# Softmax's division is applied to x as it leaves PSUM, with factors spread over rows by DMA; GpSimd takes over parts of the q and k preparation

## The chip, the cores and the metric

One core of one Trainium2 chip runs the program. Its engines are TensorE (PE in the profile; PEld is its weight load), VectorE (DVE), ScalarE (ACT), GpSimd (POOL) and SyncE (SP), which issues every DMA of this kernel. Each engine works through its own instruction queue in order and waits on semaphores. The metric is the device time of one execution in microseconds (us), as the median of several runs.

## The reference, cut to what matters

Windowed attention with a position bias is followed by a two-layer network. Batch is 8, heads 8, sequence 576, head size 64; the network has width 512, inner width 2048 and 4608 tokens. All is float32.

```python
scores = scale * np.matmul(q, k.transpose(0, 1, 3, 2))
bias = slopes[:, None, None] * (-np.abs(rel))[None, :, :]
mask = (rel >= 0) & (rel < 128)
scores = np.where(mask, scores + bias[None], -1e9)
scores = scores - np.max(scores, axis=-1, keepdims=True)
attn = np.exp(scores)
attn = attn / (np.sum(attn, axis=-1, keepdims=True) + 1e-09)
x = np.matmul(attn, v)                 # then heads side by side: 4608 x 512
h = x @ w_in
sp = np.maximum(h, 0.0) + np.log1p(np.exp(-np.abs(h)))
g = h * erf(sp)
out = g @ w_out
```

## The kernel before, in words

**Attention.** Two heads are handled together as a pair; there are 32 (batch, pair) combinations `i`. A sequence of 576 queries is cut into five tiles of 128 query rows (`QTILES`), and the tiles into two spans (`SPANS`): span w=0 holds tiles 0 to 2 (384 queries), span w=1 tiles 3 and 4 (192 queries). For the first two batches all w=0 spans come first (eight), then all w=1 spans (eight); after that both spans of a combination follow each other. There are 64 spans and 160 tiles in all.

For one tile, `scores` (line 477) lets PE multiply q and k into PSUM tile `s`, DVE adds the bias and finds the row minimum of the negated scores (L522, into `p` and into columns of the small tile `st`), and ACT takes the exponential and sums each row into other columns of `st` (L532). `p` has 128 query rows by up to 256 keys, for two heads. `normalise` (line 541) then has DVE add 1e-9 and take the reciprocal of the row sums (L549, L550; one call for a w=0 span, one call for each tile of a w=1 span), and POOL multiplies `p` by it in place, one instruction for each head (L560). PE transposes `p` in 128 x 128 blocks into PSUM tile `t` (L578), DVE or ACT copies them to SBUF as `pa` or `pb` (L472 or L474), PE multiplies with the block-diagonal v tile `vbd` into PSUM tile `px` (L596), and DVE or ACT copies `px` to `xs` (or, in the first chunks, to `xr`). There `x` stands transposed: a column is a query, rows 0 to 63 are the first head, rows 64 to 127 the second. A DMA stores it to DRAM (L642).

**Operands.** After the first four sets, q is loaded once as `qr` (L413) and k as `kr`, in two DMAs (L410). Each has one buffer, so a load waits until the last reader of the set before is done. TensorE's faster float32r product rounds its inputs, so each operand is split into a rounded high part and the low remainder: for k, `kh` on DVE or ACT (scaled by 2 to the power 2g+j, where g is the pair and j the head in it), and `kl`, the remainder, on DVE (L463); for q, the high part `a` on DVE or ACT and the remainder on POOL (L466). v comes by two DMAs (L426).

**The network.** Chunks of 384 tokens go through 16 slices of the inner width, in two passes over the tokens: slices 0 to 5 beside attention, 6 to 15 behind it. PE makes `h` (L782) and later `o` (L844), both as three products of split operands; DVE, ACT and POOL make the nonlinearity and the splits. The weights are rebuilt on chip from two 32-bit words by ACT, five DVE steps and POOL (L670 to L692). Their work tile `wq` has one buffer.

**Order.** `Plan` is a list scheduler that runs when the program is built: every operation has an engine (or a choice), an estimated cost, its dependencies and a due value `at`. Whenever an engine is free, it takes the ready operation with the smallest `at`. The estimates, with DMA latency among them, fix the order of each engine's queue; on the chip the queues run in that order and wait where something is late. SP's queue is planned in the same way.

Of the kernel before, what the change touches and what calls it, by code (L numbers as in the profile page):

```python
# [8 lines left out]
F32 = mybir.dt.float32  # L9
# [25 lines left out]
DIRECT = 2  # L35
BATCH = 1
WLO, XLO = 0, 1
# [264 lines left out]
def dve(n, fast=False):  # L302
    return 0.17 + n * (0.00056 if fast else 0.00108)
# [39 lines left out]
class Attention:  # L343


    def __init__(self, tc, plan, ctx, actx, qT, kT, vb, bias, ident, moe):
        self.nc, self.plan = tc.nc, plan
        self.qT, self.kT, self.vb = qT, kT, vb
        self.bias, self.ident, self.moe, self.spare = bias, ident, moe, (moe.ps_h, moe.ps_o)
        sb = lambda name: actx.enter_context(tc.tile_pool(name=name, bufs=1))  # L350
        ps = lambda name: ctx.enter_context(tc.tile_pool(name=name, bufs=1, space=PSUM))
        self.raw, self.split, self.pp, self.ptp, self.xsb = (
            sb(n) for n in ("raw", "split", "pp", "ptp", "xsb")
        )
        self.ps = ps("ps_a")
        vpool = sb("vpool")
        self.vbd = []
        for i in range(2):
            t = vpool.tile([P, 9, P], F32, tag=f"vbd{i}", name=f"vbd{i}")
            v = Buf(shape=[P, 9, P], ap=t)  # L360
            plan.op({"Pool": 1.2}, lambda e, t=t: self.nc.gpsimd.memset(t, 0.0), w=[v], at=-1)
            self.vbd.append(v)
        self.order = [(b, g) for b in range(B) for g in range(NPAIR)]
        self.step = self.loads = 0
        self.seq = 0
        self.warm_up()

        for w in range(2):
            for i in range(2 * NPAIR):
                self.span(i, w, self.operands(i, w), self.values(i, 4 * w, 6 + 3 * w))  # L370
        for i in range(2 * NPAIR, len(self.order)):
            operands, v = self.operands(i), self.values(i, 0, 9)
            for w in range(2):
                self.span(i, w, operands, v)
# [64 lines left out]
    def parts(self, nm, g, q, k, nq, nk, at):  # L439
# [8 lines left out]

        def scaled(e, out, src, by):
            if e == "DVE":  # L450
                nc.vector.tensor_scalar(out, src, by, None, op0=ALU.mult)
            else:
                nc.scalar.mul(out, src, by)

        either = lambda n: {"DVE": dve(n, True), "Act": act(n)}
        for j in range(2):
            own, other = (lo, hi) if j == 0 else (hi, lo)
            by = 2.0 ** (2 * g + j)
            op(either(nk), lambda e, j=j, by=by: scaled(e, kh[j][:, :nk], k[:, j, :nk], by),
               r=[k], w=[kh[j]], at=at)  # L460
            op(either(nq), lambda e, j=j, own=own: self.copy(e, a[j][own, :nq], q[own, :nq]),
               r=[q], w=[a[j]], at=at)
            op({"DVE": dve(nk)}, lambda e, j=j, by=by: nc.vector.scalar_tensor_tensor(  # L463
                kl[j][:, :nk], k[:, j, :nk], by, kh[j][:, :nk], op0=ALU.mult, op1=SUB),
                r=[k, kh[j]], w=[kl[j]], at=at)
# [74 lines left out]

    def normalise(self, i, ts, p, st, totals, at):

        nc, op = self.nc, self.plan.op
        m = P
        k = [2 * (t % 3) for t in ts]
        both = lambda: st[:m, 6 + k[0] : 8 + k[-1]]

# [3 lines left out]

        sums = [totals[t] for t in ts]
        op({"DVE": 0.5}, inverse, r=sums, w=sums, at=at)
        for t in ts:
            _, c0, c1 = QTILES[t]

            def scaled(e, t=t, c0=c0, c1=c1):
                for j in range(2):
                    dst = p[t][:m, c0:c1, j, :]
                    nc.gpsimd.tensor_scalar(  # L560
                        dst, dst, totals[t][:m, j : j + 1], 1.0, op0=ALU.mult, op1=ALU.mult
                    )

            n = (c1 - c0) * 64
            op({"Pool": 2 * pool_ts(n)}, scaled, r=[p[t], totals[t]], w=[p[t]], at=at)

# [38 lines left out]
    def span(self, i, w, operands, v):  # L605
        b, g = self.order[i]
        op = self.plan.op
        tiles, base, end, banks, _, order = SPANS[w]
# [3 lines left out]
        for t in tiles:  # L612
# [4 lines left out]
            self.step += 1  # L617
            if not (BATCH and w == 0):
                self.normalise(i, [t], p, st, totals, at)
        if BATCH and w == 0:  # L620
            self.normalise(i, tiles, p, st, totals, at)
        at += LT
# [13 lines left out]
        else:  # L636
            xs = Buf(self.xsb, [P, n], F32, f"xs{w}", 1, f"xs{i}_{w}")
        op({"DVE": dve(n), "Act": act(n, src=0.13)},
           lambda e: self.copy(e, xs.all, px[:, :n]), r=[px], w=[xs], at=at + 0.1)
        xd = Part(self.moe.x_dram[c], slice(None), g, slice(off, off + n))  # L640
# [5 lines left out]
class Weights:  # L646
# [9 lines left out]
    def prepare(self, which, f, at, after=()):  # L656
        nc, op = self.nc, self.plan.op
        nm = f"{'io'[which]}{f}"
        raw = Buf(self.stage, [P, DM, 2], I32, "wr", 2, f"wr{nm}")
        q = Buf(self.stage, [P, DM], I32, "wq", 1, f"wq{nm}")  # L660
        t = Buf(self.stage, [P, DM], I32, "wt", 2, f"wt{nm}")
# [213 lines left out]
def tile_kernel(ctx, tc, qT, kT, vb, w_in, w_out, bias, out, nb=B):  # L875
# [20 lines left out]
    actx = ctx.enter_context(ExitStack())  # L896
    Attention(tc, plan, ctx, actx, qT, kT, vb, bias_sb, ident, moe)
    ops = list(plan.ops)
# [69 lines left out]
```

## Time and profile before

| | before |
|---|---|
| median of 3 runs | 1116.12 us (1114.69 to 1117.51) |
| the profiled execution's own time | 1118.25 us |
| its span in the trace | 1116.3 us |
| mean granted TensorE clock | 0.983 |
| PE busy | 1073.7 us (96%) |
| DVE busy | 684.9 us (61%) |
| ACT busy | 721.9 us (65%) |
| POOL busy | 385.7 us (35%) |
| share of the chain that ended last | PE 82%, DVE 9%, POOL 3%, DMA 2% |

Busy time is an average over the span. Attention and the first pass end at about 520 us, and the engines other than PE are much less loaded after that. "Granted clock" is the share of its full clock at which TensorE was allowed to run in a stretch.

### The profile page before, as it was taken

What the parts mean: (1) busy time and instruction counts of PE and PEld (TensorE: products, weight loads), DVE (VectorE), ACT (ScalarE), POOL (GpSimd) and SP (SyncE); (2) the same over time, 40 slices, a digit from 0 to 9 for tenths busy, and PEclk for the clock granted to TensorE, in tenths of its full rate; (3) what the DMA queues carried; (4) which work ended last, traced back from release to release, by engine and by line L of the source; (5) the groups of instructions that cost most, each with busy time, mean ns of one, the idle gap of its engine ahead of it and who ended that gap; (6) DMA issues with size and microseconds to landing.
All of it is one profiled execution on the core that took longest, in us unless ns stands there. A gap on an engine that the chain in (4) does not pass through costs nothing.

```text
span 1116.3 us, 17069 instructions
## 1 busy us (share of the span) xinstructions
PE 1073.7 (96%) x6000; PEld 976.5 (87%) x6000; DVE 684.9 (61%) x1602; ACT 721.9 (65%) x1436; POOL 385.7 (35%) x464
## 2 busy tenths in 40 slices
PE   9776979999999999999999999999999999999998
PEld 8666968988899999999899998899999999999996
DVE  5878898887888888775867675333433433433332
ACT  6567667878788787776677675355455455455462
POOL 5776887646666566653333231000000000000000
PEclk9797999999999999999999999999999999999999
DMA  6444555444545455422343422202202202202102
GB/s 184 139 132 122 140 152 153 146 132 115 163 118 135 121 143 149 118 89 78 114 132 114 141 69 74 86 13 73 85 19 67 85 19 67 85 13 73 57 19 67
DMA packets 89732, 111.59 MB, mean 100 GB/s; under 512 B 45744, under 2 KB 59696, under 8 KB 89648
## 3 DMA queue, kind: packets, MB, share of 16 engines
q1 hardware_dynamic: 89648, 110.52, 33.5%
q8 instruction: 47, 0.77, 0.3%
q14 instruction: 37, 0.30, 0.1%
HBM read 82.18 MB, written 28.31 MB: 99 GB/s over the span
## 4 chain that ended last, share of the span: by engine, by line
PE 82%; DVE 9%; POOL 3%; DMA 2%; issue 2%; ACT 2%; POOLq 0%; SPq 0%; DVEq 0%; ACTq 0%
PE o L844 32%; PE h L782 31%; PE px L596 7%; PE s L511 5%; PE t L578 5%; POOL p L560 2%; DMA xr<-xd 2%; DVE p L522 1%; PE warm_ps L383 1%; DVE xl L759 1%; POOL wto L686 1%; DVE hs L824 1%; DVE gl L829 1%; PE s L497 1%; ACT p L532 1%
## 5 line engine op out<-in xcount | busy, mean ns | idle before, releaser
L782 PE MATMUL h<-xh,whi 128*128 128x384 f32 x768 | 262.5, 342 | 0.0
L782 PE MATMUL h<-xl,whi 128*128 128x384 f32 x768 | 259.2, 338 | 1.6 <-DVE xl L759 1.6
L782 PE MATMUL h<-xh,wli 128*128 128x384 f32 x768 | 259.7, 338 | 0.0
L560 POOL TENSOR_SCALAR p<-p,st 128x256 f32<-128x256 f32 (+2 forms) x320 | 194.0, 623 | 128.1 <-DVE st L550 108.1
L844 PE MATMUL o<-who,gh 128*128 128x512 f32 x576 | 228.8, 397 | 0.6 <-DVE ot L768 0.6
L844 PE MATMUL o<-who,gl 128*128 128x512 f32 x576 | 227.6, 395 | 1.2 <-DVE gl L829 1.2
L844 PE MATMUL o<-wlo,gh 128*128 128x512 f32 x576 | 227.3, 395 | 1.2 <-POOL wlo L692 0.7
L766 ACT COPY hs<-h 128x384 f32<-128x384 f32 x137 | 65.3, 477 | 215.1 <-PE h L782 214.6
L532 ACT ACTIVATE p<-p,st 128x256 f32<-128x256 f32 (+2 forms) x320 | 149.0, 468 | 24.5 <-DVE st L522 23.6
L782 PEld LDWEIGHTS h<-xl,whi 128*128 128x128 f32 x768 | 145.2, 189 | 8.7 <-DVE xl L759 2.1
L782 PEld LDWEIGHTS h<-xh,whi 128*128 128x128 f32 x768 | 145.3, 189 | 6.9 <-ACT hs L766 0.2
L782 PEld LDWEIGHTS h<-xh,wli 128*128 128x128 f32 x768 | 144.8, 189 | 0.2 <-POOL wli L692 0.2
L844 PEld LDWEIGHTS o<-who,gl 128*128 128x128 f32 x576 | 108.1, 188 | 25.4 <-DVE gl L829 2.1
L522 DVE CUSTOM_DVE_ANT_0 p<-s,bias_sb 128x256 f32<-128x256 f32 (+2 forms) x320 | 109.4, 378 | 33.4 <-PE s L511 21.6
L768 DVE COPY hs<-h 128x384 f32<-128x384 f32 x55 | 30.4, 554 | 160.8 <-PE h L782 160.8
L844 PEld LDWEIGHTS o<-wlo,gh 128*128 128x128 f32 x576 | 108.5, 188 | 17.9 <-POOL wlo L692 2.2
L844 PEld LDWEIGHTS o<-who,gh 128*128 128x128 f32 x576 | 108.6, 188 | 16.6 <-DVE ot L768 1.5
L824 DVE TENSOR_TENSOR hs<-s,hs 128x768 f32<-128x768 f32 x96 | 95.2, 1016 | 23.4 <-ACT s L813 23.4
L829 DVE TENSOR_TENSOR gl<-hs,gh 128x768 fp32r<-128x768 f32 x96 | 94.6, 989 | 15.5 <-ACT gh L766 14.7
L578 PE MATMUL t<-ident,p 128*128 128x128 f32 x544 | 85.7, 284 | 17.6 <-POOL p L560 11.8
L578 PEld LDWEIGHTS t<-ident,p 128*128 128x128 f32 x544 | 65.6, 147 | 30.4 <-POOL p L560 14.6
L466 POOL TENSOR_TENSOR a_None<-qr_None,a_None 64x576 fp32r<-64x576 f32 x48 | 76.4, 1592 | 25.7 <-DVE a_None L474 20.7
(80 smaller groups left out, 1653.1 us busy)
## 6 DMA issues: line engine op xcount, KB each, us to landing
xr<-xd SPq DMA_DIRECT2D x22, 768.0 KB, 4.3
kr_None<-k_t SPq DMA_DIRECT2D x48, 288.0 KB, 4.2
pd<-ot SPq DMA_DIRECT2D x36, 256.0 KB, 3.7
ot<-pd SPq DMA_DIRECT2D x36, 256.0 KB, 3.0
wri<-w_in SPq DMA_DIRECT2D x16, 512.0 KB, 3.8
wro<-w_out SPq DMA_DIRECT2D x16, 512.0 KB, 3.7
out_dram<-ot SPq DMA_DIRECT2D x32, 256.0 KB, 2.1
qr_None<-q_t SPq DMA_DIRECT2D x24, 288.0 KB, 3.1
```

What stands on the lines that cost most here:

```text
L466: op({"Pool": pool_tt(nq)}, lambda e, j=j, own=own, other=other: nc.gpsimd.tensor_tensor(a[j][other, :nq], q[own, :nq], a[j][own, :nq], SU ...
L511: nc.tensor.matmul(ps[:m, j, :n], lhsT=a[j][:, q0 : q0 + m], rhs=rhs[:, k0 : k0 + n], start=(o == 0), stop=(o == 1),)
L522: nc.vector.tensor_tensor_reduce(out=pt[:m, c0:c1, j, :], in0=blocks(src[j][0][:m, src[j][1], :n]), in1=blocks(self.bias[:m, c0 * 64 : c1 ...
L532: nc.scalar.activation(dst, dst, AF.Exp, bias=low[:m, j : j + 1], scale=-1.0, accum_out=total[:m, j : j + 1],)
L560: nc.gpsimd.tensor_scalar(dst, dst, totals[t][:m, j : j + 1], 1.0, op0=ALU.mult, op1=ALU.mult)
L578: nc.tensor.matmul(ps[:, col : col + P], lhsT=p[t][:, kb].rearrange("p j d -> p (j d)"), rhs=self.ident[:, :], is_transpose=True, start=no ...
L596: self.nc.tensor.matmul(dst[:, q0 - base : q1 - base], lhsT=v[:, blk], rhs=sb[sbi][:, off : off + q1 - q0], start=(blk == order[0][0]), st ...
L766: self.nc.scalar.copy(out, src)
L782: nc.tensor.matmul(ps[:, :CH], lhsT=ww[:, cs], rhs=xx[:, k], start=(k2 + k + n == 0), stop=(k2 + k + n == 4),)
L824: V if e == "DVE" else G).tensor_tensor(hs[:, :n], s[:, :n], hs[:, :n], ALU.mult),
L829: V if e == "DVE" else G).tensor_tensor(gl[:, :n], hs[:, :n], gh[:, :n], SUB),
L844: nc.tensor.matmul(po.all, lhsT=g[:, j, cs], rhs=w.all, start=(u["start"] and n == 0), stop=(u["end"] and n == 2),)
```

## The change

Five things change together.

1. `normalise` goes. POOL's 320 multiplications of `p` are gone; `p` is transposed and multiplied with v as the bare exponential.
2. `inverses` takes its place, once for each span: DVE adds 1e-9 and takes the reciprocal of all the span's row sums. The factors stand in `st` with the query on the partition, and are needed with the query along the row. One SP DMA for each tile writes them to a new DRAM tensor `rd` of 2 rows (heads) by n queries; two more read each head's row back, repeated on 64 partitions, into `rs`. That is 5 DMAs for a w=0 span and 4 for a w=1 span, 288 in all, and the readback waits for the write.
3. The copy of `px` out of PSUM becomes a multiplication of `px` by `rs`, on DVE only.
4. The power-of-two scale of k moves to q: POOL multiplies `qr` in place by a column `heads` (1 or 2 by head) and by 4 to the power g. `kh` becomes a plain copy, and `kl` a plain subtraction that moves from DVE to POOL.
5. `wq` gets a second buffer.

```diff
-BATCH = 1
+RB = 2
...
+        self.heads = Buf(sb("heads"), [P, 1], F32, "heads", 1, "heads")
+        for j in range(2):
+            plan.op({"Pool": 0.2}, lambda e, j=j: self.nc.gpsimd.memset(
+                self.heads[j * D : (j + 1) * D], 2.0**j), w=[self.heads], at=-1)
...
+        op({"Pool": pool_ts(nq)}, lambda e: nc.gpsimd.tensor_scalar(
+            q[:, :nq], q[:, :nq], self.heads[:, 0:1], 4.0**g, op0=ALU.mult, op1=ALU.mult),
+           r=[q, self.heads], w=[q], at=at)
...
-            op(either(nk), lambda e, j=j, by=by: scaled(e, kh[j][:, :nk], k[:, j, :nk], by),
+            op(either(nk), lambda e, j=j: self.copy(e, kh[j][:, :nk], k[:, j, :nk]),
                r=[k], w=[kh[j]], at=at)
...
-            op({"DVE": dve(nk)}, lambda e, j=j, by=by: nc.vector.scalar_tensor_tensor(
-                kl[j][:, :nk], k[:, j, :nk], by, kh[j][:, :nk], op0=ALU.mult, op1=SUB),
+            op({"Pool": pool_tt(nk)}, lambda e, j=j: nc.gpsimd.tensor_tensor(
+                kl[j][:, :nk], k[:, j, :nk], kh[j][:, :nk], SUB),
                 r=[k, kh[j]], w=[kl[j]], at=at)
...
-    def normalise(self, i, ts, p, st, totals, at):
+    def inverses(self, i, w, st, totals, at):
...
-                    nc.gpsimd.tensor_scalar(
-                        dst, dst, totals[t][:m, j : j + 1], 1.0, op0=ALU.mult, op1=ALU.mult
-                    )
+        rd = Buf(ap=self.dram.tile([2, n], F32, name=f"rd{i}_{w}"))
+        rs = Buf(self.xsb, [P, n], F32, f"rs{w}", RB, f"rs{i}_{w}")
+        def out(e):
+            for t in tiles:
+                q0 = max(QTILES[t][0], base + P * (t % 3))
+                p0 = q0 - QTILES[t][0]
+                k = 6 + 2 * (t % 3)
+                nc.sync.dma_start(
+                    rd[:, q0 - base : q0 - base + P - p0].rearrange("j q -> q j"),
+                    st[p0:P, k : k + 2])
+        def back(e):
+            for j in range(2):
+                nc.sync.dma_start(rs[j * D : (j + 1) * D], rd[j : j + 1].broadcast_to([D, n]))
+        op(emit=out, r=sums, w=[rd], at=at, **dma(2 * n * 64, len(tiles), 0.6))
+        op(emit=back, r=[rd], w=[rs], at=at, **dma(P * n * 4, 2, 0.6))
...
-        op({"DVE": dve(n), "Act": act(n, src=0.13)},
-           lambda e: self.copy(e, xs.all, px[:, :n]), r=[px], w=[xs], at=at + 0.1)
+        op({"DVE": dve(n)}, lambda e: nc.vector.tensor_tensor(xs.all, px[:, :n], rs.all, ALU.mult),
+           r=[px, rs], w=[xs], at=at + 0.1)
...
-        q = Buf(self.stage, [P, DM], I32, "wq", 1, f"wq{nm}")
+        q = Buf(self.stage, [P, DM], I32, "wq", 2, f"wq{nm}")
```

More of the change, by code (lines that the diff above doesn't have):

```diff
@@ L343, with __init__ @@
 class Attention:
-    def __init__(self, tc, plan, ctx, actx, qT, kT, vb, bias, ident, moe):
-        self.nc, self.plan = tc.nc, plan
+    def __init__(self, tc, plan, ctx, actx, qT, kT, vb, bias, ident, moe, dram):
+        self.nc, self.plan, self.dram = tc.nc, plan, dram
         self.qT, self.kT, self.vb = qT, kT, vb
@@ L447, in parts @@
         kl = [Buf(self.split, [P, S], F32R, f"kl{j}", 2, f"kl{nm}_{j}") for j in range(2)]
[L449 to L453, printed above, removed]
+        op({"Pool": pool_ts(nq)}, lambda e: nc.gpsimd.tensor_scalar(
+            q[:, :nq], q[:, :nq], self.heads[:, 0:1], 4.0**g, op0=ALU.mult, op1=ALU.mult),
+           r=[q, self.heads], w=[q], at=at)
         either = lambda n: {"DVE": dve(n, True), "Act": act(n)}
@@ L457, in parts @@
             own, other = (lo, hi) if j == 0 else (hi, lo)
-            by = 2.0 ** (2 * g + j)
-            op(either(nk), lambda e, j=j, by=by: scaled(e, kh[j][:, :nk], k[:, j, :nk], by),
+            op(either(nk), lambda e, j=j: self.copy(e, kh[j][:, :nk], k[:, j, :nk]),
                r=[k], w=[kh[j]], at=at)
@@ L539, in scores @@
         return pt
-    def normalise(self, i, ts, p, st, totals, at):
+    def inverses(self, i, w, st, totals, at):
         nc, op = self.nc, self.plan.op
-        m = P
-        k = [2 * (t % 3) for t in ts]
-        both = lambda: st[:m, 6 + k[0] : 8 + k[-1]]
+        tiles, base, end, *_ = SPANS[w]
+        n = end - base
+        both = lambda: st[:, 6 : 6 + 2 * len(tiles)]
         def inverse(e):
@@ L550, in inverse @@
             nc.vector.reciprocal(both(), both())
-        sums = [totals[t] for t in ts]
+        sums = [totals[t] for t in tiles]
         op({"DVE": 0.5}, inverse, r=sums, w=sums, at=at)
[L554 to L560, printed above, removed]
-                        dst, dst, totals[t][:m, j : j + 1], 1.0, op0=ALU.mult, op1=ALU.mult
-                    )
-            n = (c1 - c0) * 64
-            op({"Pool": 2 * pool_ts(n)}, scaled, r=[p[t], totals[t]], w=[p[t]], at=at)
+        rd = Buf(ap=self.dram.tile([2, n], F32, name=f"rd{i}_{w}"))
[13 more added lines that the diff above has]
+        op(emit=back, r=[rd], w=[rs], at=at, **dma(P * n * 4, 2, 0.6))
+        return rs
     def transpose_bank(self, i, w, bi, p, sb, at):
@@ L606, in span @@
         b, g = self.order[i]
-        op = self.plan.op
+        nc, op = self.nc, self.plan.op
         tiles, base, end, banks, _, order = SPANS[w]
@@ L617, in span @@
             self.step += 1
[L618 to L621, printed above, removed]
+        rs = self.inverses(i, w, st, totals, at)
         at += LT
@@ L896, in tile_kernel @@
     actx = ctx.enter_context(ExitStack())
-    Attention(tc, plan, ctx, actx, qT, kT, vb, bias_sb, ident, moe)
+    Attention(tc, plan, ctx, actx, qT, kT, vb, bias_sb, ident, moe, dram)
     ops = list(plan.ops)
```

## The prediction

> **What bounds the kernel now.** I read the page first: PE is busy nearly everywhere but in the first tenths of the span.
>
> ```profile
> span 1116.3 us, 17069 instructions
> ...
> PE   9776979999999999999999999999999999999998
> ```
>
> Then the stages. Columns are stretch, length, busy time of PE, PEld, DVE, ACT and POOL (with instructions), granted clock, DMA share, GB/s.
>
> ```profile
> 0.00:50.00 50.00, 43.09 (x275) 37.82 (x275) 35.17 (x126) 31.92 (x100) 31.92 (x54) 0.90 0.56 161
> 50.00:100.00 50.00, 40.47 (x232) 37.02 (x232) 39.05 (x128) 32.67 (x90) 34.40 (x47) 0.86 0.50 138
> 100.00:150.00 50.00, 40.42 (x235) 36.81 (x235) 43.41 (x114) 37.67 (x90) 39.35 (x38) 0.90 0.49 131
> 150.00:200.00 50.00, 44.68 (x274) 40.22 (x273) 44.94 (x112) 33.61 (x92) 39.40 (x40) 0.97 0.58 161
> 200.00:250.00 50.00, 47.98 (x307) 44.15 (x306) 41.84 (x124) 40.68 (x100) 28.58 (x37) 1.00 0.48 133
> ```
>
> PE idles 6.9 + 9.5 + 9.6 + 5.3 + 2.0 = 33.4 us here. Its clock is granted at 0.90, 0.86, 0.90 and 0.97 in the first four rows, worth at most 43.1 x 0.10 + 40.5 x 0.14 + 40.4 x 0.10 + 44.7 x 0.03 = 15.4 us. After 250 us PE is all but full, and the change leaves its instructions as they are. So at most 33.4 + 15.4 = 48.8 us can be won, all before 250 us; there a microsecond of idle PE moves the end by about one, since PE's work behind it is fixed. DVE is the fullest other engine: 43.4 and 44.9 of 50 us from 100 to 200. PE's own waits over the whole span (engine and line, awaited, us in total, times, longest):
>
> ```profile
> PE s L511 <- DVE st L522: 12.5, 13, 2.0
> PE t L578 <- POOL p L560: 11.8, 7, 5.4
> ```
>
> The transposes wait for POOL's normalisation, the scores for DVE's bias step to free `s`. The first wait is what the change takes away.
>
> **The change part by part: POOL.** Groups by shape of before (busy us, mean ns, idle before):
>
> ```profile
> L560 POOL TENSOR_SCALAR p<-p,st 128x256 f32<-128x256 f32 x192 | 124.6, 665 | 7.4 <-DVE st L550 5.6 <-ACT p L532 1.0 <-ACT a_None L472 0.4
> L466 POOL TENSOR_TENSOR a_None<-qr_None,a_None 64x576 fp32r<-64x576 f32 x48 | 76.4, 1592 | 25.7 <-DVE a_None L474 20.7 <-ACT a_None L472 1.2 <-POOL p L560 1.0
> L560 POOL TENSOR_SCALAR p<-p,st 128x192 f32<-128x192 f32 x64 | 41.6, 660 | 8.9 <-ACT p L532 5.9 <-DVE st L550 1.9 <-DVE st L522 0.4
> L560 POOL TENSOR_SCALAR p<-p,st 128x128 f32<-128x128 f32 x64 | 28.9, 462 | 111.8 <-DVE st L550 100.7 <-ACT p L532 9.5 <-ACT xh L766 1.4
> ...
> L466 POOL TENSOR_TENSOR a<-qr,a 64x192 fp32r<-64x192 f32 x16 | 12.9, 805 | 12.8 <-DVE wqi L678 4.2 <-DVE a L474 3.1 <-ACT a L472 2.2
> ```
>
> Removed: 124.6 + 41.6 + 28.9 = 195.1 us. Added: 72 `kl` subtractions, priced by L466: 48 of 576 columns at 1.592; the slope (1592 - 805) / 384 = 2.05 ns a column gives 1.07 for 16 of 320 and 1.20 for 8 of 384; together 76.4 + 17.1 + 9.6 = 103.1 us. 36 scalings of q: the slope of L560 from 128 to 256 columns, 1.59 ns, gives 1.17 for 24 of 576 and 0.87 for 4 of 384; the row has 0.66 for 8 of 192; together 36.9 us. POOL falls from 385.7 to 330.6 us, so it does not become the bound. What becomes late is another thing: `p` no longer passes through it, the operands pass through it more.
>
> **DVE and ACT.** Groups of all shapes:
>
> ```profile
> L463 DVE SCALAR_TENSOR_TENSOR kl_None<-kr_None,kh_None 128x576 fp32r<-128x576 f32 x48 | 43.2, 906 | 0.1
> ...
> L549 DVE TENSOR_SCALAR st<-st 128x2 f32<-128x2 f32 (+1 forms) x96 | 28.2, 294 | 3.1 <-ACT p L532 2.8
> ...
> L550 DVE RECIPROCAL st<-st 128x2 f32<-128x2 f32 (+1 forms) x96 | 16.7, 174 | 3.3
> ...
> L463 DVE SCALAR_TENSOR_TENSOR kl<-kr,kh 128x320 fp32r<-128x320 f32 (+1 forms) x24 | 12.8, 550 | 1.9 <-ACT kh L453 1.8
> L472 ACT COPY xs<-px 128x192 f32<-128x192 f32 (+1 forms) x32 | 12.3, 384 | 28.9 <-PE px L596 22.6 <-ACT p L532 1.9 <-issue 1.9
> ...
> L474 DVE COPY xs<-px 128x192 f32<-128x192 f32 (+1 forms) x24 | 10.7, 447 | 12.3 <-PE px L596 12.3
> ```
>
> DVE loses 43.2 + 12.8 = 56.0 us of `kl` and 32 of 96 reciprocal pairs, 32 x 0.468 = 15.0 us. It gains the 32 exits of x that ACT did, 32 x 0.447 = 14.3 us, if the multiplication costs what the copy did; no row shows it, and at half or double the price DVE's 64 exits would come to 14 us less or 29 us more. I take the copy's, which has the same PSUM source. Net about -57 us, a tenth of DVE's work before 520 us. ACT loses 12.3 us. `kh` as a copy instead of a scaling, `wq`'s second buffer and two memsets of `heads` cost nothing: the first keeps its engines, the second only takes a wait off ACT, the third run in the first microseconds, when POOL has no tile; without that cover they are two instructions.
>
> **SP and the factors' trip.** 288 DMAs are new. SP's queue for one w=1 span now (start, length):
>
> ```profile
> 75.78 0.33 SPq L413 DMA_DIRECT2D qr<-q_t  x1
> 77.20 1.26 SPq L410 DMA_DIRECT2D kr<-k_t  x2
> 78.50 1.27 SPq L426 DMA_DIRECT2D vbd<-v_b  x2
> 79.87 0.55 SPq L642 DMA_DIRECT2D xd<-xs  x1
> 81.69 0.33 SPq L413 DMA_DIRECT2D qr<-q_t  x1
> ```
>
> One issue costs 0.33 to 0.63 us. The time from issue to landing (min/median/max), first for the stores `xd`, then for the v loads, whose pieces are the smallest of before:
>
> ```profile
> DMA to landing us min/median/max: 1.6/2.7/6.9
> ```
>
> ```profile
> DMA to landing us min/median/max: 2.3/3.0/5.1
> ```
>
> No row has pieces of 4 bytes. The trip of a w=0 span is two issues ahead of the last write, its landing, one issue ahead of the last readback, its landing: 2 x 0.63 + 3.0 + 0.63 + 2.7 = 7.6 us by medians, 2 x 0.33 + 1.6 + 0.33 + 1.6 = 4.2 by the least, 1.26 + 5.1 + 0.63 + 6.9 = 13.9 by the most. For w=1 one issue less, 7.0 us. I take the medians. The Trainium skill (DMA: Bandwidth & Descriptors, Specifications) speaks against the write: below 512 B the engines read, modify and write. By that rule the write would come nearer to the 5.1 us than to 3.0, and the trip to 9.7; no run here shows it yet.
>
> The cover is the time from a span's reciprocal to the exit of its x. Here are two spans; DVE's queue first, then the exit of the second on ACT:
>
> ```profile
> 35.31 0.19 DVE L550 RECIPROCAL st<-st 128x6 f32<-128x6 f32 x1
> ...
> 46.38 0.56 DVE L474 COPY xr<-px 128x384 f32<-128x384 f32 x1 [1.45 <-PE px L596]
> ...
> 64.47 0.19 DVE L550 RECIPROCAL st<-st 128x6 f32<-128x6 f32 x1
> ```
>
> ```profile
> 73.52 0.48 ACT L472 COPY xr<-px 128x384 f32<-128x384 f32 x1 [0.19 <-PE px L596]
> ```
>
> 11.1 and 9.1 us. Without POOL's six instructions between (6 x 0.462 = 2.8 us) the products could end that much sooner, leaving 6.3 to 8.3 us against a trip of 7.0 to 7.6. So the trip is about hidden, with little to spare. If it is late, DVE stands at the multiplication, and behind it in its queue wait the bias steps (PE's `s`), the weight steps and the splits. `px` is held too, but the next products are a span away.
>
> **The sum**, against the profiled 1118.25 us (span 1116.3 and 1.95 around it; 2.1 above the median):
> - PE's wait for POOL at the transposes: 11.8 us go, but ACT's exponentials and the copies out of `t` are next; I take two thirds, -8 (bounds -11.8 and 0).
> - DVE a tenth lighter: of the 12.5 us that scores wait for it, -2 (bounds -8 and +2).
> - Clock: with 10 of 33.4 us of gaps gone, about that share of 15.4: -4 (bounds -15 and 0).
> - The trip: about 30 of the 64 spans (250 us of the 520 that attention takes) have no full PE to hide behind; 0.2 us each at DVE, half of it reaching PE: +3 (bounds 0 and +25, below).
> - Operands: `qr` has one buffer and its next load waits for POOL:
>
> ```profile
> SPq L413 <- POOL a L466: 9.1, 5, 4.7
> ```
>
> That is of the first 110 us. A w=1 set now holds POOL 2 x 0.805; with two `kl` and the scaling it is 2 x 1.07 + 0.66 = 2.8 us more, while POOL loses 2 x 0.665 + 2 x 0.660 = 2.65 of `p` for each such span. Bounds 0 and 12 split sets x 2.8 = +34; nearest is even, +2.
>
> Together -9: 1109 for this execution, **1107** as a median.
>
> **The rivals.** (a) More is won, about 1092: a lighter DVE, which is 88% full from 100 to 200, lets the weights come sooner and half of the 48.8 us goes. For it: DVE's rows. Against: PE's two waits shown are 24.3 of its gaps, and neither is for weights. (b) No change, about 1115: -8 is eaten by the operands' cycle, since `qr` and `kr` free late and SP's loads behind them too; the +34 bound shows room, POOL's even balance speaks against it. (c) Slower, about 1132: the factors come late. SP's rows add up to 3.4 us of issues a w=1 span, in the 5.9 us between the two q loads shown; four more DMAs make up to 5.9, so SP is full and anything that waits in front of a readback delays it. It decides from a trip of about 8.3 us, the longer cover. At 10 us, 1.7 over, 30 spans and half reaching PE cost 25 us: 1107 + 25 = 1132. The skill's read-modify-write rule points here. Against: from 250 us on PE's backlog hides it. (d) That division is not moved at all can be left out, since the code does it unconditionally.
>
> **How the numbers follow.** Forecast 0.46, (a) 0.16, (b) 0.13, (c) 0.25. Within 0.3%, about 3.3 us, a measurement of this kernel can't be told from no change. The forecast's own range is 1099 to 1112, so faster 0.62, same 0.13, slower 0.25. The range goes down to 1088, past (a), and up to 1132, which leaves half of (c) out.
>
> **What would show it.** Right: PE's transposes no longer wait for POOL but for little on ACT; PE idle in the first 250 us near 24 us; the clock of 50 to 150 us above 0.9; DVE near 628 us and POOL near 331; landing times of the `rd` write near 3 us; DVE's wait for the readback under 10 us in all. Wrong: DVE waiting for the `rs` DMA by tens of us, or SP's queue standing in front of it, or scores waiting for POOL's `kl`.

## The result, and the profile after

The changed kernel takes 1501.66 us (median of 4 runs, 1498.53 to 1503.86) against 1116.20: a ratio of 1.345 with a 95% interval of 1.342 to 1.348. It is slower by 385 us, where 1107 was forecast. The page of after, its engines, PE's slices and the chain that ended last:

```profile
span 1500.8 us, 17200 instructions
...
PE 1167.1 (78%) x6000; PEld 1051.2 (70%) x6000; DVE 691.6 (46%) x1520; ACT 698.9 (47%) x1382; POOL 328.8 (22%) x254
...
PE   6556655586766667666476589989999999999998
...
PE 41%; DMA 11%; DVE 2%; issue 1%; ACT 1%; SPq 1%; POOL 0%; DVEq 0%; ACTq 0%; POOLq 0%
```

PE executes the same 6000 instructions. The spans differ by 1500.8 - 1116.3 = 384.5 us. PE's busy time rose by 1167.1 - 1073.7 = 93.4 us, and its idle time from 1116.3 - 1073.7 = 42.6 to 1500.8 - 1167.1 = 333.7 us, which is 291.1 more; the two make up the whole. On the chain that ended last the DMAs have 11%, where they had 2%. The longer busy time goes with the granted clock, as the stretches of after show (columns as in the prediction's table of stages):

```profile
0.00:250.00 250.00, 149.80 (x775) 133.58 (x776) 135.61 (x362) 104.31 (x278) 103.20 (x104) 0.77 0.58 100
250.00:500.00 250.00, 167.94 (x900) 149.39 (x899) 113.45 (x333) 100.08 (x277) 72.00 (x53) 0.83 0.61 95
500.00:750.00 250.00, 155.92 (x864) 141.79 (x862) 100.79 (x298) 102.66 (x261) 65.26 (x45) 0.81 0.59 84
750.00:1000.00 250.00, 197.39 (x987) 178.51 (x988) 147.31 (x286) 130.57 (x237) 74.56 (x46) 0.85 0.38 90
1000.00:1250.00 250.00, 250.00 (x1257) 226.65 (x1256) 104.90 (x131) 135.00 (x174) 13.73 (x7) 1.00 0.18 61
```

In the first four stretches PE is 60 to 79% busy and its clock is granted at 0.77 to 0.85; from 1000 us on PE is busy throughout and the clock is at 1.00. The missing shares of the clock come to 149.80 x 0.23 + 167.94 x 0.17 + 155.92 x 0.19 + 197.39 x 0.15 = 122 us, some 107 more than the 15 of before, which is about the 93 us of longer busy time. No engine is near its limit in the first 750 us. The waits of after (engine and line, awaited, us in total, times, longest us):

```profile
POOL qr_None L453 <- DMA qr_None<-q_t: 221.6, 18, 21.3
DVE xs L643 <- DMA rs<-rd: 211.2, 41, 13.6
...
PE px L604 <- DVE xs L643: 158.2, 30, 12.9
PE s L511 <- DVE st L522: 98.4, 31, 13.6
...
DVE xr L643 <- DMA rs<-rd: 22.8, 5, 7.2
```

DVE stands 234 us before the multiplication of x by its factors; PE stands 158 us because `px` isn't free, and 98 for the bias steps, which stand behind that multiplication in DVE's queue. POOL waits about as long, 222 us, for the loads of q. On SP's own queue one large wait is new (the largest, 402 us for finished outputs, was there before with 374):

```profile
SPq L569 <- DMA rd<-st: 351.0, 65, 10.2
```

Here are two spans of after in SP's timeline (start, length of the issue), and then the piece of the chain of waits that goes with them:

```profile
658.35 1.18 SPq L563 DMA_DIRECT2D rd<-st  x2
659.58 0.59 SPq L417 DMA_DIRECT2D qr_None<-q_t  x1
667.60 1.09 SPq L569 DMA_DIRECT2D rs<-rd  x2
668.78 0.53 SPq L647 DMA_DIRECT2D xd<-xs  x1
669.42 1.48 SPq L563 DMA_DIRECT2D rd<-st  x3
670.95 1.25 SPq L430 DMA_DIRECT2D vbd<-v_b  x2
680.24 0.34 SPq L753 DMA_DIRECT2D xr<-xd  x1
680.68 0.38 SPq L647 DMA_DIRECT2D xd<-xs  x1
681.25 1.11 SPq L569 DMA_DIRECT2D rs<-rd  x2
```

```profile
670.44 10.74 DMA rd<-st
...
681.77 10.67 DMA rs<-rd
...
692.53 0.57 DVE xs L643
```

The three writes are issued from 669.42, the readback is issued at 681.25, and the factors are there at 681.77 + 10.67 = 692.44: a trip of 23.0 us, where at most 13.9 had been reckoned with. It is a long one: the rows of the division alone, shown further down, give about 14 by their medians. In the span ahead of it SP issues nothing from 660.17 to 667.60: it stands in front of the readback, and the store of x, the next writes and the loads of v planned behind it wait too.

### The profile page after: what moved, and what is told of

The parts are those of the page before. It is cut to its first block, busy times and chain, and to the rows that moved or that the text cites. A ratio compares the mean times of both kernels' runs of the same rounds, so it can differ in the third digit from the quotient of the medians.

```text
span 1500.8 us, 17200 instructions
## 1 busy us (share of the span) xinstructions
PE 1167.1 (78%) x6000; PEld 1051.2 (70%) x6000; DVE 691.6 (46%) x1520; ACT 698.9 (47%) x1382; POOL 328.8 (22%) x254
## 4 chain that ended last, share of the span: by engine, by line
PE 41%; DMA 11%; DVE 2%; issue 1%; ACT 1%; SPq 1%; POOL 0%; DVEq 0%; ACTq 0%; POOLq 0%
PE o L849 20%; PE h L787 19%; DMA rd<-st 8%; DMA rs<-rd 3%; PE px L604 1%; PE s L511 1%; SPq L569 0%; SPq L563 0%; DVE gl L834 0%; PE t L586 0%; DVE wti L678 0%; DVE xs L643 0%; ACT p L532 0%; DVE p L522 0%; DVE hs L829 0%
## 5 line engine op out<-in xcount | busy, mean ns | idle before, releaser
L787 PE MATMUL h<-xh,wli 128*128 128x384 f32 x768 | 266.7, 347 | 12.3 <-POOL wli L697 12.2
L787 PE MATMUL h<-xh,whi 128*128 128x384 f32 x768 | 270.7, 352 | 3.5 <-DVE xh L773 3.5
L787 PE MATMUL h<-xl,whi 128*128 128x384 f32 x768 | 265.9, 346 | 0.6 <-DVE xl L764 0.6
L849 PE MATMUL o<-who,gh 128*128 128x512 f32 x576 | 236.0, 410 | 6.6 <-DVE ot L773 6.6
L604 PE MATMUL px<-pb,vbd 128*128 128x64 f32 (+2 forms) x320 | 72.1, 400 | 137.7 <-DVE xs L643 136.7
L604 PEld LDWEIGHTS px<-pb,vbd 128*128 128x128 f32 x320 | 67.5, 290 | 147.3 <-DVE xs L643 145.8
L511 PE MATMUL s<-kh_None,a_None 128*128 128x256 f32 (+2 forms) x240 | 75.8, 334 | 84.8 <-DVE st L522 82.6
L643 DVE TENSOR_TENSOR xs<-px,rs 128x192 f32<-128x192 f32 (+1 forms) x56 | 24.8, 442 | 239.9 <-DMA rs<-rd 211.2
L511 PEld LDWEIGHTS s<-kh_None,a_None 128*128 128x128 f32 x240 | 52.9, 220 | 95.3 <-issue 66.5
L604 PE MATMUL px<-pa,vbd 128*128 128x192 f32 (+2 forms) x384 | 78.0, 356 | 50.7 <-DVE xs L643 21.5
```

The source lines that it names most:

```text
L511: nc.tensor.matmul(ps[:m, j, :n], lhsT=a[j][:, q0 : q0 + m], rhs=rhs[:, k0 : k0 + n], start=(o == 0), stop=(o == 1),)
L604: self.nc.tensor.matmul(dst[:, q0 - base : q1 - base], lhsT=v[:, blk], rhs=sb[sbi][:, off : off + q1 - q0], start=(blk == order[0][0]), st ...
L643: op({"DVE": dve(n)}, lambda e: nc.vector.tensor_tensor(xs.all, px[:, :n], rs.all, ALU.mult), r=[px, rs], w=[xs], at=at + 0.1)
L787: nc.tensor.matmul(ps[:, :CH], lhsT=ww[:, cs], rhs=xx[:, k], start=(k2 + k + n == 0), stop=(k2 + k + n == 4),)
L849: nc.tensor.matmul(po.all, lhsT=g[:, j, cs], rhs=w.all, start=(u["start"] and n == 0), stop=(u["end"] and n == 2),)
```

## The experiments

Fifteen kernels were run: first the change's parts, then what in the trip costs so much, then how small pieces in DRAM behave, and at last the parts together. Ratios are to the kernel before on the same chip, with 95% intervals.

### The parts: trip, operands, `wq`, normalisation

**Without the trip.**

```diff
-        op(emit=out, r=sums, w=[rd], at=at, **dma(2 * n * 64, len(tiles), 0.6))
-        op(emit=back, r=[rd], w=[rs], at=at, **dma(P * n * 4, 2, 0.6))
+        rs = self.one        # a constant tile of ones, [128, 384]
```

> The changed kernel without the factors' trip: no write to DRAM and no readback; DVE still makes the reciprocals, and x leaves PSUM multiplied by a constant tile of ones (so x is not divided by the row sums; all else is computed). Theory T, the trip (SP stood 351 us in front of the readbacks, and DVE 234 us in front of the multiplications): the time falls to about the forecast, 1100 to 1115 us. Rival O, the operands (kl and the scaling of q on POOL, one buffer each for q and k): it stays above 1400 us.

Measured 1140.96 us, ratio 1.0212 (1.0193 to 1.0230). So the 288 DMAs are worth 1501.66 - 1140.96 = 361 us of the loss. But what is left is still 24 us slower than before, above the 1100 to 1115 us expected, so the change loses without its trip as well. DVE, which should have become a tenth lighter, is busy for 707.4 us (684.9 before).

**The division alone**: the trip stays, q and k are prepared as before.

```diff
-        op({"Pool": pool_tt(nk)}, lambda e, j=j: nc.gpsimd.tensor_tensor(...))   # kl
+        op({"DVE": dve(nk)}, lambda e, ...: nc.vector.scalar_tensor_tensor(...))
         # and kh scaled on DVE or ACT, no scaling of q, no heads
```

> The changed kernel with the q and k preparation of before (the scale in kh and in kl, kl on DVE, no scaling of q on POOL); the trip stays. Theory T: about 1480 to 1510 us, nearly nothing comes back. Rival O: at most 1150 us.

Measured 1498.11 us, ratio 1.3412 (1.3364 to 1.3460), not told apart from the whole change. While the factors are late, it doesn't matter where the operands are made.

**No trip, operands of before**, the same undoing as in the last diff on top of the first.

> No trip (x leaves PSUM multiplied by ones, not divided), and the q and k preparation of before (kl on DVE, scale in kh and kl). With what is left of the change: POOL's 320 multiplications gone, fewer reciprocals, x's exit on DVE, wq's second buffer. If kl and the scaling on POOL cost the 24 us by which the kernel without a trip was slower than before (POOL's long instructions hold up DVE's short ones, where the rows show casts of a going from 458 to 1171 ns at the median), this is 1095 to 1115 us. If the 24 us come from somewhere else (the exit on DVE, the order of the weights), it stays above 1130 us.

Measured 1127.02 us, ratio 1.0096 (1.0061 to 1.0131), which lies between the two expectations. Without the trip the operands on POOL cost 1140.96 - 1127.02 = 14 us, and 10 of the 24 come from somewhere else. Here are the casts that make q's high part, on DVE (min/median/max ns), without the trip with the new operands, and then with the old ones:

```profile
L476 DVE CAST a_None<-qr_None x33: 420/1171/1658, 137.7 to 495.0; 64x576 fp32r<-64x576 f32 x33
```

```profile
L476 DVE CAST a_None<-qr_None x21: 441/456/1556, 138.2 to 483.3; 64x576 fp32r<-64x576 f32 x21
```

At the median the same instruction takes 1.17 us instead of 0.46. The two traces show why. Without the new operands, 18 of the 21 casts run beside no working instruction of POOL and last 0.44 to 0.46 us; the other three start behind one and last 1.52 to 1.56. With them, 22 of the 33 start while a two-input subtraction of POOL is running, and each of these ends 0.31 to 0.32 us after that subtraction does; the other 11 start ahead of a subtraction or beside none, and last 0.42 to 0.46 us. So a cast that starts second stands until POOL's instruction is done. The Trainium skill (SBUF — State Buffer, SBUF: two separate sides) says that VectorE and GpSimd share a pair of ports to SBUF as an exclusive lock held for a whole instruction, for VectorE's instructions in a two-port mode or with two inputs in SBUF; the lengthened casts agree with the lock, and which mode they run in is not shown.

With `kl` gone from DVE the planner also gave DVE more casts (33 instead of 21), so DVE's queue won nothing. And scores have a wait on POOL that the run with the old operands does not have, for the remainder of q (L468, without the trip):

```profile
PE s L513 <- POOL a L468: 6.0, 5, 2.4
...
PE s L513 <- POOL a_None L468: 3.3, 2, 2.0
```

No run separates the longer casts from the longer chain of POOL's own steps, so how the 14 us are shared between them is not shown.

**`wq`'s second buffer alone**, put into the kernel before:

```diff
-        q = Buf(self.stage, [P, DM], I32, "wq", 1, f"wq{nm}")
+        q = Buf(self.stage, [P, DM], I32, "wq", 2, f"wq{nm}")
```

> The kernel of before with a second wq buffer and nothing else. I priced this edit at nothing. If the order of the weights that it allows is what leaves 10 us between the kernel without trip and with the operands of before (1127 us) and before (1116.5), this is 1121 to 1130 us; if not, 1112 to 1119 us.

Measured 1127.17 us, ratio 1.0094 (1.0062 to 1.0126): a buffer more costs 10 us. Three of its stretches after attention:

```profile
550.00:600.00 50.00, 46.45 (x223) 40.96 (x224) 46.78 (x62) 30.88 (x42) 28.34 (x17) 0.97 0.39 130
600.00:650.00 50.00, 47.72 (x235) 41.88 (x234) 45.02 (x58) 31.96 (x45) 28.25 (x15) 1.00 0.39 132
650.00:700.00 50.00, 50.00 (x253) 45.33 (x252) 18.17 (x23) 25.97 (x34) 0.00 (x0) 1.00 0.14 48
```

and the same of before:

```profile
550.00:600.00 50.00, 49.04 (x247) 44.24 (x247) 37.56 (x53) 34.55 (x46) 15.44 (x11) 1.00 0.39 127
600.00:650.00 50.00, 50.00 (x256) 45.72 (x255) 34.45 (x53) 36.11 (x48) 16.83 (x12) 1.00 0.37 123
650.00:700.00 50.00, 49.93 (x254) 45.20 (x253) 28.88 (x45) 28.18 (x36) 10.97 (x8) 1.00 0.22 69
```

With two buffers the weights of the second pass are rebuilt in one bunch: DVE is 46.78 and 45.02 us busy of 50 and then only 18.17, and PE idles 3.6 + 2.3 us in the first two stretches where it had idled 1.0. That is about half of the 10 us; the stretch ahead of them, 500 to 550 us, has 2.4 more (2.9 against 0.5). The single buffer had spread that work.

**No trip, operands of before, one `wq`**: what is left is that `normalise` is gone, the reciprocals are joined and x leaves PSUM by a multiplication on DVE, by ones.

> The run without trip and with the operands of before (1127 us; x is not divided), with one wq buffer as before. What is left of the change is that POOL no longer multiplies p, fewer reciprocals, and x's exit on DVE alone. If wq's buffer costs the 10 us, this is 1105 to 1119 us, and shows what the removal of the normalisation is worth at best. If the exit on DVE or the fuller DVE costs them, it stays at 1122 to 1130 us.

Measured 1116.07 us (10 runs), ratio 0.9986 (0.9971 to 1.0001). `wq` is confirmed: 1127.02 - 1116.07 = 11 us. And the change's one gain, 195 us of POOL's work taken away, is with the two small edits beside it worth about 1.6 us, and at the interval's end 3.2. PE's largest wait in this run:

```profile
PE s L513 <- DVE st L524: 22.2, 17, 4.6
```

Before, scores waited 12.5 us for DVE and transposes 11.8 for POOL. The wait for POOL is gone, and PE's gaps have not shrunk: 1117.0 - 1069.0 = 48.0 us over the span, where they were 42.6. Waits for DVE and ACT, which were next, have its place, and PE's busy time is 4.7 us shorter.

From this kernel the whole way can be walked by one edit at a time: 1116.1, with the second `wq` 1127.0, with the operands on POOL 1141.0, with the trip 1501.7. It is one order of the edits; with the trip first, the operands would add only the 3 us or so of the second run.

### The trip: who waits for what

**Nobody waits for the writes.** They are issued as in the change, but the readback takes a constant row of DRAM, so no instruction needs what they write.

```diff
-                nc.sync.dma_start(rs[...], rd[j : j + 1].broadcast_to([D, n]))
+                nc.sync.dma_start(rs[...], self.rc[j : j + 1, :n].broadcast_to([D, n]))
```

> The changed kernel, with all writes of 4-byte pieces issued but waited for by nobody: the readbacks fetch ones from a DRAM tensor that was written once at the start (x is not divided), at the same place after the reciprocals, and the multiplication waits for them. If the loss is SP standing in its queue until a write has landed, with the loads behind it, the time falls below 1250 us (1141 us without a trip, and up to 100 for readbacks that run behind the pieces in the DMA queues). If the loss is the traffic of the pieces itself, which every load shares, it stays above 1350 us.

Measured 1474.34 us, ratio 1.3199 (1.3141 to 1.3258). SP's 351 us in front of the readback are gone, and 27 us are won. So it isn't that wait alone. The waits of this run:

```profile
POOL qr_None L458 <- DMA qr_None<-q_t: 241.1, 18, 22.6
DVE xs L648 <- DMA rs<-rc: 235.7, 48, 11.1
```

DVE now waits for a transfer whose data have lain in DRAM since the start. What is left of the writes is that they share SP's queue and the DMA engines with everything else. SP isn't rid of them altogether: the profile puts 104.6 us of its waits, 46 of them, down to such a write landing, in front of other DMAs (the largest 26.3 us, in front of the next writes). With the pieces 64 bytes apart, further down, no such wait is left. Why one DMA's issue waits for another's landing is not shown.

**Nobody waits for the readback.** The whole trip is made, x is multiplied by ones.

```diff
-           lambda e: nc.vector.tensor_tensor(xs.all, px[:, :n], rs.all, ALU.mult), r=[px, rs]
+           lambda e: nc.vector.tensor_tensor(xs.all, px[:, :n], self.one[:, :n], ALU.mult), r=[px, self.one]
```

> The changed kernel, whole trip issued, readback waiting for its write on SP as before, but the multiplication takes a constant tile of ones (x is not divided), so DVE and px wait for no factor. If DVE standing at the multiplication is the loss (234 us of waits in the changed kernel, 171 us of PE behind them), the time falls below 1250 us. If SP standing in front of the readbacks with the operand loads behind it is enough by itself, it stays above 1350 us.

Measured 1487.33 us, ratio 1.3315 (1.3264 to 1.3366). DVE's wait for the factors is gone and 14 us are won; SP waits 372.5 us for the writes, and the loads behind them come late:

```profile
POOL qr_None L455 <- DMA qr_None<-q_t: 130.6, 15, 23.7
DVE kh_None L476 <- DMA kr_None<-k_t: 89.4, 14, 13.2
```

Neither wait is the cause by itself. Each takes the place of the other, as long as the writes are there.

**The planner is told.** The same instructions, but the write is planned as landing 8 us later and the readback 3 us later than its estimates had it.

```diff
-        op(emit=out, r=sums, w=[rd], at=at, **dma(2 * n * 64, len(tiles), 0.6))
-        op(emit=back, r=[rd], w=[rs], at=at, **dma(P * n * 4, 2, 0.6))
+        op(emit=out, r=sums, w=[rd], at=at, late=8.0, **dma(2 * n * 64, len(tiles), 0.6))
+        op(emit=back, r=[rd], w=[rs], at=at, late=3.0, **dma(P * n * 4, 2, 0.6))
```

> The changed kernel, but the list scheduler is told that the write takes 8 us longer to land and the readback 3 us longer, as the trace shows, so it puts other loads in front of the readback and the multiplication later in DVE's queue. Same instructions in another order. If the loss is mostly the order (an estimate that was 3 to 5 times too short, and in-order queues), the time falls below 1250 us. If the trip is simply too long and its traffic too heavy for this loop, it stays above 1400 us.

Measured 1371.90 us, ratio 1.2282 (1.2242 to 1.2322). That is between the two times expected. A better order wins 130 us: SP now waits 33.4 us for the writes instead of 351. The other 231 us of the trip's 361 stay.

### Small pieces side by side

A write of the change moves 128 query rows by 2 heads from SBUF, one 4-byte piece from each partition for each head, into two stretches of 512 bytes in DRAM (32 of the 160 writes move 64 rows).

**As rows.** PE transposes the columns of `st`, DVE or ACT copies them out of PSUM, and one write of two rows takes the place of two or three writes of pieces; the readback is as it was.

```diff
+                nc.tensor.matmul(ft[:2, o : o + P], lhsT=st[:, k : k + 2], rhs=self.ident[:, :],
+                                 is_transpose=True, start=True, stop=True)
+        op({"DVE": dve(n), "Act": act(n, src=0.13)},
+           lambda e: self.copy(e, fr[:, :n], ft[:2, :n]), r=[ft], w=[fr], at=at)
...
-                nc.sync.dma_start(rd[...].rearrange("j q -> q j"), st[p0:P, k : k + 2])
+            nc.sync.dma_start(rd.all, fr[:, :n])
```

> The changed kernel, but TensorE first turns the factors (one 128-column transpose for each tile, 160 in all, some 17 us of PE by the row of the p transposes), DVE or ACT copies them to two rows, and one DMA a span writes two rows of 1536 or 768 bytes in place of two or three DMAs of 4-byte pieces. Readback as before. If the size of the pieces is what makes the write late, it lands in 2 to 3 us and the time is 1110 to 1150 us. If any write and dependent readback through DRAM takes 8 to 10 us here, it stays above 1400 us.

Measured 1153.01 us, ratio 1.0317 (1.0300 to 1.0334). The same factors go the same way through DRAM and are waited for by the same instructions, and 349 of the 361 us are gone. It is the write in small pieces, then, and not the trip as such. The number of writes fell too, from 160 to 64; the runs with pieces apart, below, keep it.

**Half the pieces**: as in the run whose writes nobody waits for, with the factors of one head only.

```diff
-                    rd[:, q0 - base : q0 - base + P - p0].rearrange("j q -> q j"),
-                    st[p0:P, k : k + 2])
+                    rd[0:1, q0 - base : q0 - base + P - p0].rearrange("j q -> q j"),
+                    st[p0:P, k : k + 1])
```

> As the run with unwaited writes (1474 us), but only the first head's factors are written: 128 pieces of 4 bytes a DMA in place of 256 (x is not divided). If the count of pieces sets the loss, this is near the run with 128 pieces of 8 bytes, 1220 to 1270 us; if the size of a piece matters by itself (4 bytes slower than 8), it stays above 1300 us.

Measured 1436.57 us, ratio 1.2853 (1.2762 to 1.2943): half as many pieces win 38 us of the 333 between 1474 and 1141. The loss doesn't go with their number.

**Pieces of 8 bytes**: the two heads of a query side by side, 128 pieces a write, which are waited for and read back as in the change (the readback then gives the factors in another order).

```diff
-        rd = Buf(ap=self.dram.tile([2, n], F32, name=f"rd{i}_{w}"))
+        rd = Buf(ap=self.dram.tile([n, 2], F32, name=f"rd{i}_{w}"))
```

> The changed kernel, but the DRAM tensor holds the two heads' factors of a query side by side, so a write is 128 pieces of 8 bytes in place of 256 of 4. The readback has the shape it had, so the factors arrive in another order (x is divided by the wrong sums). If the time of a write goes by its number of pieces, SP's wait in front of the readbacks halves, from 351 us to about 175, and the time falls to 1250 to 1350 us. If it goes by the DMA (or by the bytes), both stay.

Measured 1244.45 us (one run, so without an interval). As many pieces as in the run before, packed as closely, and 192 us less.

**Pieces apart**: again with writes that nobody waits for, all 256 pieces of 4 bytes, each 512 bytes from the next; then 64 bytes, then 16.

```diff
-        rd = Buf(ap=self.dram.tile([2, n], F32, name=f"rd{i}_{w}"))
+        rd = Buf(ap=self.dram.tile([2, n, 128], F32, name=f"rd{i}_{w}"))   # or 16, or 4
...
-                    rd[:, q0 - base : q0 - base + P - p0].rearrange("j q -> q j"),
+                    rd[:, q0 - base : q0 - base + P - p0, 0].rearrange("j q -> q j"),
```

> As the run with unwaited writes (1474 us; readbacks fetch ones from a DRAM tensor written once, so x is not divided), but every 4-byte piece goes to a place of its own in DRAM, 512 bytes from the next, in place of packed rows where neighbouring pieces come from different DMA engines. If pieces are slow because neighbours share a stretch of DRAM, the time falls below 1300 us. If it is the count of pieces, it stays within 30 us of 1474.

> As the run with pieces 512 bytes apart (1161.9 us), with 64 bytes from one 4-byte piece to the next; the writes are waited for by nobody and the readback is of a constant, so x isn't divided by its row's own sum. Theory of a stretch of 64 bytes or less, within which neighbouring pieces hold each other up: nothing is shared any more, 1155 to 1175 us. Rival, a stretch of 512 bytes: eight pieces still share one, as eight-byte pieces packed in 64 bytes would, 1240 to 1350 us. Rival, that the spread over much memory is what helps (512 bytes apart covers 128 KB a write, 64 apart 16 KB): something between, 1180 to 1240 us.

> The same with 16 bytes from piece to piece, x again not divided by its row's own sum. Stretch of 64 bytes: four pieces share one, 1180 to 1260 us. Stretch of 512 bytes: 32 pieces share one, 1400 to 1480 us, near the packed pieces (1474.3 us). Stretch of 16 bytes or less: 1155 to 1175 us.

| 4-byte pieces, unwaited | median | ratio (95%) |
|---|---|---|
| packed | 1474.34 | 1.3199 (1.3141 to 1.3258) |
| 16 bytes apart | 1202.68 | 1.0758 (1.0697 to 1.0819) |
| 64 bytes apart | 1158.86 | 1.0366 (1.0317 to 1.0415) |
| 512 bytes apart | 1161.93 | 1.0396 (1.0362 to 1.0430) |

With 64 bytes between them, as many pieces, as small, through the same queue, cost 1158.86 - 1140.96 = 18 us instead of 333, the readbacks included. From 64 to 512 bytes nothing more is won, so it isn't the spread over more memory, and 16 bytes still cost 44 us more than 64. The plainest reading is that pieces hold each other up within a stretch of DRAM that is longer than 16 bytes and not longer than 64. The DMA rows (tensors, issues, KB each, median us from issue to landing), first of the division alone, which makes the trip as the change does:

```profile
kr_None<-k_t SPq DMA_DIRECT2D x48, 288.0 KB, 7.9
...
rs<-rd SPq DMA_DIRECT2D x64, 96.0 KB, 2.9
rs<-rd SPq DMA_DIRECT2D x64, 48.0 KB, 3.2
rd<-st SPq DMA_DIRECT2D x128, 1.0 KB, 9.3
```

8-byte pieces:

```profile
kr_None<-k_t SPq DMA_DIRECT2D x48, 288.0 KB, 6.3
...
rd<-st SPq DMA_DIRECT2D x128, 1.0 KB, 5.0
```

4 bytes, 16 apart:

```profile
kr_None<-k_t SPq DMA_DIRECT2D x48, 288.0 KB, 5.2
...
rd<-st SPq DMA_DIRECT2D x128, 1.0 KB, 4.1
```

4 bytes, 64 apart:

```profile
kr_None<-k_t SPq DMA_DIRECT2D x48, 288.0 KB, 4.3
...
rd<-st SPq DMA_DIRECT2D x128, 1.0 KB, 2.5
```

One kilobyte takes 9.3, 5.0, 4.1 or 2.5 us by where its pieces lie, and a load of k, which has nothing to do with it, 7.9, 6.3, 5.2 or 4.3 (4.2 in the kernel before). The first two runs wait for their writes and the last two don't. The two unwaited runs with packed pieces and with 64 bytes between them can be compared by their DMA queue (packets, MB, the time of the packets as a share of 16 engines' span):

```profile
q1 hardware_dynamic: 139316, 120.13, 41.4%
```

```profile
q1 hardware_dynamic: 139316, 120.13, 38.4%
```

The same packets take 0.414 x 1475.6 x 16 = 9774 us packed and 0.384 x 1153.8 x 16 = 7089 us apart. In the traces a 4-byte packet itself takes 9 ns at the median in both. The others lengthen: a packet of 2304 bytes, one row of q or k, takes 218 ns on average beside packed pieces and 137 beside pieces apart.

The time from issue falls with the number of pieces that share 64 bytes (16, 8, 4, 1); a stretch of 32 bytes would put the runs in the same order. That they are serialised there, each read, changed and written back in turn, would fit, and the Trainium skill (DMA: Bandwidth & Descriptors, Specifications) has a read-modify-write below 512 B. But 4-byte pieces far apart are below 512 B as well and land in 2.5 us: the rule alone isn't the price, the neighbours are. How the chip arranges them was not seen in any trace, and whether it matters that neighbouring pieces come from different partitions was not tried.

### The parts together

**Rows, operands of before, one `wq`.** The form with rows, and the two other losses taken back.

> The division still by the trip, but the factors go out as two long rows that PE turned; q and k prepared as before, one buffer for wq. Theory that the three parts of the loss add up: 1153.0 - 14 (operands) - 10 (second wq buffer) = 1129 us, ratio 1.011. Rival, that the operands' and the buffer's losses only stood behind free engines and the trip's own waits (58.7 us of SP's, 12.7 us of DVE's) then decide: no gain, 1145 to 1153 us. Rival, that the idea pays once its losses are away: 1113 us or less.

Measured 1157.75 us, ratio 1.0362 (1.0325 to 1.0399): the parts don't add up, and taking 14 + 10 us back wins nothing here. Compared with the kernel that has no trip and is otherwise the same (1116.07), the trip as rows costs 42 us; with the new operands and two buffers it had cost 1153.01 - 1140.96 = 12. The groups of its turning matmuls and of its second product of the network (busy us, mean ns, idle before):

```profile
L857 PE MATMUL o<-who,gh 128*128 128x512 f32 x576 | 231.1, 401 | 7.2 <-DVE who L701 7.2
...
L565 PE MATMUL ft<-ident,st 128*2 128x128 f32 x160 | 29.0, 281 | 14.8 <-DVE st L551 14.1 <-ACT pb L472 0.6
```

PE spends 29.0 us on the turns (17 had been expected for them), waits 14.8 in front of them, and 7.2 for weights that come late. Against the kernel without a trip, PE's busy time rises by 1096.1 - 1069.0 = 27.1 us and its gaps from 48.0 to 1155.8 - 1096.1 = 59.7. With the new operands and two buffers, busy time rose by 1095.1 - 1078.1 = 17.0 us and the gaps fell, from 1141.0 - 1078.1 = 62.9 to 1153.4 - 1095.1 = 58.3. Where PE had waited for its operands anyway, part of the turns lay in its gaps; here it didn't. That reading is from the profiles alone; why busy time rose by 27 here and by 17 there stays open.

No form of the idea that was run beats the kernel before, and the run without any trip shows why none can be expected to: with the factors free and the side edits taken back it is within 0.3% of it.

## Why the prediction was wrong

**What bounds the kernel, and the room.** Right: PE, with 33.4 us of gaps before 250 us. The room was there, and the change used none of it: PE idles 250 - 149.80 = 100.2 us in the first 250 us of after, where 24 had been named as the sign.

**PE's wait for POOL (-8), lighter DVE (-2), clock (-4).** The step failed where two thirds of the 11.8 us were taken as won. The run with nothing but this shows -1.6 us (-3.2 to 0). PE is busy for 214.4 of its first 250 us, so it idles 35.6 against 33.4: the transposes don't wait for POOL any more, as foretold, but scores wait 22.2 us for DVE instead of 12.5. The bound of 0 was near the value; the next wait behind the removed one was as long.

**Operands (+2, bound +34).** Mis-sized: +14 without the trip. The balance on POOL came out (328.8 us busy, 331 foretold), but by luck: in after the subtractions and scalings take 124 us instead of the 140 of the sum, and POOL's steps for the weights 107 instead of 91, which the sum had left out. The price lay on DVE, where the sum had put a gain: foretold 628 us, measured 707.4 without the trip and 691.6 in after. Two steps of the argument were missing: the planner fills a lighter DVE with casts that ACT had made, and a cast that starts behind one of POOL's subtractions stands until it is done (1.17 us at the median, not 0.46). Scores now wait for POOL as well, 9.3 us. The exits' price was right (0.358 us for 192 columns and 0.558 for 384, where 0.447 had been taken on average).

**`wq`'s second buffer (0).** It failed at "only takes a wait off ACT". That wait paced the weights; without it they come in a bunch, DVE fills up and PE stands: +10 us, shown twice.

**The trip (+3, bounds 0 and +25).** This is the step that failed: +361 us. The write was priced by the v loads, 3.0 us at the median and 5.1 at the most, as the nearest rows. It takes 9.3. The prediction said that no row has pieces of 4 bytes, and then set the upper bound from rows of large pieces all the same. The figure that it drew from the rule of the Trainium skill (DMA: Bandwidth & Descriptors, Specifications) pointed the right way (nearer to 5.1), yet it is short by 4.2 us, and pieces that lie apart, to which that rule applies too, land in 2.5 us. The larger omission is that the sum charged the writes to their own trip alone: with no instruction in need of them they still cost 333 us (18 with their pieces 64 bytes apart), by what shares SP's queue and the DMA engines with them.

The cover was read a little too long as well. POOL's six instructions take 3.05 and 3.09 us in the two spans, not 2.8, and in the second POOL begins them 2.0 us after the reciprocal; with that delay gone as well, an estimate of that cover is nearer 4 us than 6.3.

**Rival (c), 1132, chance 0.25.** It named the waits that came: SP's queue is full, what stands in front of a readback delays it, DVE stands at the multiplication, `px` and the bias steps behind it. But these waits are not the cause by themselves: with SP's wait in front of the readback gone 333 us of the 361 stay, and with DVE's wait for the factors gone 346. Its price failed as well. The trip was set at 10 us; it is about 14 by the medians of the division alone (2 x 0.5 for the issues ahead, 9.3, 0.5, 2.9) and 23.0 in the span shown, where the readback itself takes 10.67. And it counted 30 spans of 64, because "from 250 us on PE's backlog hides it". The backlog never forms: PE is busy for 167.94 and 155.92 us of 250 between 250 and 750, and DVE waits for the factors in 46 of the 64 spans, up to the last exit of x at 893.8 us, where attention had ended at about 520:

```profile
L643 DVE TENSOR_TENSOR xs<-px,rs x56: 345/358/558, 144.9 to 893.8; 128x192 f32<-128x192 f32 x32, 128x384 f32<-128x384 f32 x24
```

(The multiplications by the factors in after: min/median/max ns, first and last start.) Nor did it see that the transfers of everything else slow down: POOL waits 221.6 us for q, and a load of k takes 7.9 us in the division alone, 4.2 before. The signs named as proof against the forecast (DVE waiting for `rs` by tens of us, SP standing in front of it) are the ones that came, at 234 and 351 us. Scores waiting for POOL's `kl` did not come among the large waits.

## What to carry to other kernels

A transfer of a kind that the trace doesn't show, such as 4-byte pieces written by many partitions next to each other, has no upper bound in that trace: measure one before costing a plan on it, and if it must be, write rows, or leave 64 bytes between the pieces (what it costs to read such pieces back was not run). Off-path work taken from an engine (here 195 us of POOL's) is worth what the next wait leaves, which was nothing; look for that next wait first. A single buffer, and work left on the busier engine, can be what paces or shields the others, so undo side edits one at a time before the main one is judged.

## What was not expected of the hardware

- Neighbouring small writes hold each other up, by these runs within a stretch of DRAM longer than 16 bytes and not longer than 64: 1 KB in 256 pieces lands in 9.3 us packed (in a run that waits for it) and in 2.5 us with 64 bytes between them, and the kernel takes 1474 or 1159 us with writes that nobody waits for.
- Such writes delay unrelated loads on the same DMA engines: 288 KB of k took 7.9 us instead of 4.3 from issue to landing, and a packet of 2304 bytes 218 ns instead of 137 on average, while the small packets themselves took 9 ns either way.
- With as many pieces, 8 bytes each instead of 4 made the kernel faster (1244 us, one run, against 1437): how many pieces share a stretch fits this, and how many bytes there are doesn't.
- A cast of 64 x 576 on DVE that starts while GpSimd runs a two-input subtraction ends 0.31 to 0.32 us after that subtraction; 0.46 us becomes 1.17 at the median.
- The granted clock was 0.77 to 0.85 in stretches of 250 us in which PE was 60 to 79% busy; the longer busy time that goes with it is 93 of the 385 us.
